# Batch 3's k as token blocks through the DMA's transpose: one change to a fused attention and MoE kernel

## The chip, the cores and the metric

The kernel runs on one core of a Trainium2 chip. The metric is the device time of one execution in microseconds (us). The core has five engines with queues of their own: TensorE (PE; its weight loads are shown as PEld), VectorE (DVE), ScalarE (ACT), GpSimd (POOL) and SyncE (SP), which here only issues DMAs. Each queue runs in order, and engines wait for one another through semaphores.

## What is computed

```python
def _attn_ref(q, k, v):                      # 8 batches, 8 heads, 576 tokens, 64 wide
    scores = scale * np.matmul(q, k.transpose(0, 1, 3, 2))
    rel = pos[:, None] - pos[None, :]
    bias = slopes[:, None, None] * (-np.abs(rel))[None, :, :]
    mask = (rel >= 0) & (rel < 128)
    scores = np.where(mask, scores + bias[None], -1e9)
    attn = softmax(scores)
    return np.matmul(attn, v)

def _moe_ref(x, w_in, w_out):                # 4608 tokens, 512 -> 2048 -> 512
    h = x @ w_in
    g = h * np.clip(h + 3.0, 0.0, 6.0) / 6.0
    return g @ w_out

x = attn_out.transpose(0, 2, 1, 3).reshape(B * S, H * D)
return _moe_ref(x, w_in, w_out)
```

Attention has a causal window of 128 tokens and a linear bias for each head. Its output, heads side by side, goes through two dense layers with a hard swish between them. Inputs and output are float32; the kernel computes its products in bfloat16.

## The kernel before

**Groups.** Attention is worked off in 32 groups: group g is the batch g // 4 and a pair of heads, g % 4 (`hp` in the code). For each group the 576 tokens are cut into five blocks of 128 (the last has 64), and only the scores of a block with itself (`scd`, line 324) and with the block before it (`sco`, lines 350 and 356) are computed. ScalarE takes the exponentials (lines 379, 389, 395) into `pd` and `po`, GpSimd zeroes what lies outside the mask (the selects of lines 382, 392, 398), TensorE multiplies with v (lines 411 and 419, `values`), and VectorE divides by the sums into `avs` (line 430). `back` brings the average into the layout of the dense layers, `xT`: from group 8 on by a DMA transpose that SP issues (line 466), in groups 10 and 11 and before group 8 by TensorE.

**The dense layers as filling.** The dense layers' matmuls (`hps`, line 492, and `ops`, line 547) stand in one list of units, and `fill(n)` puts the next n units between the steps of attention. All engines' orders are written out by hand: `first_batch` (groups 0 to 3), `second_batch` (4 to 7), then `segment` for groups 8 to 32. An iteration g of `segment` holds, in TensorE's order, the scores of group g, units, the averages of group g - 1 in two parts with units between and behind, and the output tiles of finished units are stored by SP (line 557). The scores of group 13 come at the end of iteration 12.

**How q and k get their layout.** The scores need q and k with the head's 64 elements on the partitions (`qTb`, `kTb`, two buffers each, by the batch's parity). There are two ways.
- *Long runs and TensorE.* `load_double` (line 98) loads four heads as runs of nine tokens for each partition (2304 bytes in one piece), in two DMAs of 288 KB; `prepare_double` (line 239) casts them to bfloat16 in two casts of 576 columns; `double` (line 254) transposes the nine pieces on TensorE, five and four, and a copy each (line 256) takes them from PSUM to `kTb`. A batch's k needs this twice (`dp` 0 and 1).
- *Token blocks and the DMA.* `load_tokens` (line 110) loads the five blocks of 128 tokens (8 heads, pieces of 256 bytes; four DMAs of 256 KB and one of 128), `cast_tokens` (line 206) casts each block on GpSimd into the shared buffer `tbuf`, and `xbar` (line 211) lets one DMA transpose of SP's write all of `qTb` or `kTb`. There is one `tbuf`, so the casts of the next tensor wait until the transpose before has read it.

Batches 0 to 2 take the first way for q and k, batches 4 to 7 the second. Batch 3 takes the second for q and the first for k. Its loads are issued by SP at the end of `second_batch`, behind v2's. v3 follows in iteration 9 (`LOADS`), q4 in iteration 10, k4 in iteration 12 and v4 in iteration 13.

**The order around the change.** `stage_next(g)` runs near the end of iteration g and prepares the next batch: it issues the loads of `LOADS`, and in the first two groups of a batch (`hp` 0 and 1) the casts on GpSimd and the transposes on SP. GpSimd's selects for group g + 1 stand behind the casts of `stage_next(g)` in its queue. In iterations 10 and 11 `turn` puts `double` for batch 3's k ahead of the first units.

The four fp32 buffers `ldbuf` are shared: k's runs of batch 3 and its token blocks after the change both lie in buffer 1, q's blocks in buffer 3, v's in buffer 0.

Of the kernel before, what the change touches and what calls it, by code (L numbers as in the profile page):

```python
# [18 lines left out]
def kernel(  # L19
# [9 lines left out]
    nc = tc.nc  # L29
    B, H, S, D = q.shape  # L30
# [5 lines left out]
    NP = H // 2  # L36
# [59 lines left out]
    def load_double(b, dp, nm, eng):  # L96
        for e in range(2):
            eng.dma_start(out=ldbuf["qk".index(nm)][:, ds((2 * dp + e) * RT * D, RT * D)],
                          in_=src_of[nm][b, ds(4 * dp, 4), :, :].rearrange(
                              "(i e) (a t) d -> e a i (t d)", e=2, t=RT)[e])  # L100
# [7 lines left out]
    def load_block(b, nm, j, eng):  # L108
        n = min(128, S - j * 128)
        eng.dma_start(out=tokens(b, nm)[:n, j, :, :],  # L110
                      in_=src_of[nm][b, :, ds(j * 128, n), :].rearrange("h p d -> p h d"))

    def load_tokens(b, nm):
        for j in range(NQ):
            load_block(b, nm, j, nc.sync)
# [79 lines left out]
    def cast_tokens(b, nm):  # L195
        s = ld[b, nm]
        if nm == "v":
            for lo in (0, 2):
                nc.gpsimd.tensor_copy(  # L199
                    out=vbuf[b % 2][:, lo:lo + 2, :, 0:D].rearrange("p j h d -> p (j h) d"),  # L200
                    in_=s[:, lo:lo + 2, :, :].rearrange("p j h d -> p (j h) d"))
            nc.gpsimd.tensor_copy(out=vbuf[b % 2][:LAST, 4, :, 0:D], in_=s[:LAST, 4, :, :])
            return
        for j in range(NQ):
            m = min(128, S - j * 128)
            nc.gpsimd.tensor_copy(out=tbuf[:m, :, j, :],  # L206
                                  in_=s[:m, j, :, :].rearrange("p (i e) d -> p i (e d)", e=2))

    def xbar(b, nm):
        dst = (qTb if nm == "q" else kTb)[b % 2]  # L210
        nc.sync.dma_start_transpose(out=dst.rearrange("p h j c -> p (h j) c"),
                                    in_=tbuf.rearrange("p h j c -> p (h j c)"))
# [22 lines left out]
    def prepare_double(b, dp, copies, nms="kq", early=None):  # L235
        for nm, copy in zip(nms, copies):
            pr = prs.tile([128, RT, 2 * D], BF16, tag=f"pr{nm}", name="pr2")
            for e in range(2):
                copy(out=pr[:, :, ts(e, D)],  # L239
                     in_=ldbuf["qk".index(nm)][:, ds((2 * dp + e) * RT * D, RT * D)].rearrange(  # L240
                         "p (t d) -> p t d", t=RT))
                if early and (nm, e) == (nms[0], 0):
                    early()
            st[b, dp, nm] = pr
# [3 lines left out]
    def double(b, dp, nm, part, tag, copy):  # L248
        src = st[b, dp, nm]
        t0, t1 = ((0, 5), (5, RT))[part]  # L250
        tp = BANKS[tag].tile([128, t1 - t0, 128], BF16, tag=tag, name="tp2",
                             padded_shape=[128, 8, 128])
        for t in range(t0, t1):
            nc.tensor.transpose(tp[:, t - t0, :], src[:, t, :], ident)  # L254
        dst = (qTb if nm == "q" else kTb)[b % 2][:, 2 * dp:2 * dp + 2, :, :]
        copy(out=dst.rearrange("p i j c -> p i (j c)")[:, :, 0:S].rearrange(
                 "p i (a t) -> p i a t", t=RT)[:, :, :, t0:t1],
             in_=tp.rearrange("p t (a i) -> p i a t", i=2))
# [54 lines left out]
    def scores_diag(g):  # L313
        rooms(g)
        b, hp = divmod(g, NP)
        qT, kT = qTb[b % 2][:, hp, :, :], kTb[b % 2][:, hp, :, :]
        first = not diag_tabled(g)
        if (g, "scd") not in st:
            tables_diag(g)
        scd = st[g, "scd"]  # L320
        for j in range(4):
            for e in range(2):
                r = slice(e * D, (e + 1) * D)
                nc.tensor.matmul(scd[:, e, ts(j, 128)], lhsT=kT[r, j, :],  # L324
                                 rhs=qT[r, j, :], start=first, stop=first or j == 3)
# [36 lines left out]
    def exp_off_full(g):  # L362
        nc.scalar.activation(out=st[g, "po"].rearrange("p e j c -> p e (j c)"),
                             in_=st[g, "sco"], func=ACT.Exp, scale=scale)
# [214 lines left out]
    V, P, A = nc.vector.tensor_copy, nc.gpsimd.tensor_copy, nc.scalar.copy  # L579
# [6 lines left out]
    def stage_next(g):  # L586
        b, hp = divmod(g, NP)
        nb = b + 1
        if g == 2 * NP:
            cast_tokens(2, "v")  # L590
        for n in LOADS.get(g, "").split():
            load_tokens(int(n[1]), n[0])
        if nb == 3 and hp < 2:
            prepare_double(3, hp, (P,), "k")
        if nb == 3 and hp == 1:
            cast_tokens(3, "q")
            xbar(3, "q")
        elif nb < B and nb > 3 and hp < 2:
            cast_tokens(nb, "qk"[hp])
            xbar(nb, "qk"[hp])  # L600
        if VCAST.get(g):
            cast_tokens(VCAST[g], "v")
# [76 lines left out]
    def second_batch():  # L679
        scores_diag(NP + 0)  # L680
        exp_diag(NP + 0, 0)
        exp_diag(NP + 0, 1)
        fill(2)
        scores_off(NP + 0)
        exp_off_full(NP + 0)
        wide_double(1, 1, "k", V)
        fill(1)
        wide_double(1, 1, "q", V)
        fill(1)
        scores_diag(NP + 1)  # L690
        exp_diag(NP + 1, 0)
        exp_diag(NP + 1, 1)
        fill(2)
        scores_off(NP + 1)
        exp_off_full(NP + 1)
        fill(1)
        cast_tokens(1, "v")
        scores_diag(NP + 2)
        exp_diag(NP + 2, 0)
        exp_diag(NP + 2, 1)  # L700
        fill(1)
        scores_off(NP + 2)
        exp_off_full(NP + 2)
        fill(2)
        for i in range(0, 4):
            load_w_out(i)
        g = 2 * NP - 1
        scores(g)
        exp_diag(g, 0)
        exp_diag(g, 1)  # L710
        prepare_double(2, 0, (V, P))
        prepare_double(2, 1, (P, P))
        nc.gpsimd.memset(ldbuf[2][:, 0:1], 0.0)
        load_tokens(2, "v")
        for dp in range(2):
            load_double(3, dp, "k", nc.sync)
        load_tokens(3, "q")
        exp_off_full(g)
        fill(1)
        attend(NP)  # L720
        fill(1)
        attend(NP + 1)
        fill(1)
        back(NP)
        attend(NP + 2)
        fill(1)
        back(NP + 1)
        double(2, 0, "k", 0, "av", A)
        attend(NP + 3)
        back(NP + 2)  # L730
        double(2, 0, "k", 1, "av", A)
        wide_double(2, 0, "q", A)
        up_begin(1, 0, 3)
        back(2 * NP - 1)
        up_begin(1, 1, 3)
        done[0] = 2 * NP
        fill(2)
        scores_diag(2 * NP)
        scores_off(2 * NP)
# [3 lines left out]
    def segment(lo, hi, fills):  # L743
        for g in range(lo, hi + 1):
            f = fills(g)
            if by_xbar(g - 2):
                done[0] = g - 1
            if lo < g < hi and g != 3 * NP + 1:
                scores(g)
            turn = {2 * NP: (2, 1, "k"), 2 * NP + 1: (2, 1, "q"),  # L750
                    2 * NP + 2: (3, 0, "k"), 2 * NP + 3: (3, 1, "k")}.get(g)
            if turn:
                double(*turn, 0, "av", A)
            fill(f[0])
            if turn:
                double(*turn, 1, *(("h", V) if turn[0] == 2 else ("av", A)))
            if g < hi:
                exp_diag(g, 0)
            fill(f[1])
            if g < hi:  # L760
                exp_diag(g, 1)
            if g == 3 * NP:
                cast_tokens(3, "v")
            if g > lo:
                values(g - 1, (0, 1, 2))
            fill(f[2])
            if g < hi:
                exp_off(g, 0)
            fill(f[3])
            if g < hi:  # L770
                exp_off(g, 1)
            if g > lo:
                values(g - 1, (3, 4))
            fill(f[4])
            if g > lo and by_xbar(g - 1):
                back(g - 1)
            fill(f[5])
            if g < hi:
                stage_next(g)
            fill(1)  # L780
            if g == 3 * NP:
                scores(g + 1)
            if g > lo and not by_xbar(g - 1):
                back(g - 1)
                done[0] = g
            fill(f[6] - 1)
# [49 lines left out]
```

## Time and profile before

| | |
|---|---|
| median of 3 runs | 323.95 us (323.73 to 324.63) |
| span of the profiled execution | 321.8 us |
| TensorE busy | 308.2 us, 96% |
| ScalarE busy | 196.0 us, 61% |
| VectorE busy | 175.5 us, 55% |
| GpSimd busy | 138.4 us, 43% |
| granted TensorE clock | 0.9 or more in every slice |
| DMA packets | 131426, of which 118977 under 512 bytes |

The profile is that of one execution, and its span is some 2 us shorter than the median of the times, since what lies ahead of the first instruction and behind the last is not in it. Busy times overlap: their sum says nothing, and matmuls are pipelined, so that TensorE's busy time is no measure of how well it is used. A DMA has three times: when SP begins to issue it, when SP is done issuing (only then does SP go on to the next), and when its data has landed. The chain that ended last is followed back from the last instruction and tells which work set the end of this execution; it doesn't tell how close another chain was.

### The profile page before, as it was taken

Reading aid. Unit: us, or ns where it says so; the run is one execution under the profiler, and the core shown is the slowest. Engines: PE = TensorE matmul, PEld = TensorE weight load, DVE = VectorE, ACT = ScalarE, POOL = GpSimd, SP = SyncE. Lnnn points to the kernel's source line nnn. Section 1 sums busy time; section 2 is a strip of 40 time slices with the busy share of each in tenths; the row PEclk is TensorE's granted clock in tenths of the full one; section 3 lists DMA queues with packets and bytes.
Section 4 is the critical chain, followed back from the end, with each engine's and each line's share of the span. In section 5 each row is a group of like instructions: output and inputs, shape, how many; then the busy total and the mean of one; then the engine's idle time right before and its main releaser. Section 6 shows DMA issues by size and latency. Waiting matters only on the chain.

```text
span 321.8 us, 6865 instructions
## 1 busy us (share of the span) xinstructions
PE 308.2 (96%) x2620; PEld 164.6 (51%) x2659; DVE 175.5 (55%) x346; ACT 196.0 (61%) x337; POOL 138.4 (43%) x247
## 2 busy tenths in 40 slices
PE   6888999999999999999999999999999999999996
PEld 3564465455555545455667655455454444444443
DVE  6686595564346655555555556554655455445510
ACT  3857977877777766766676667666764344244401
POOL 7364590665494767446654663663331000000000
PEclk9999999999999999999999999999999999999999
DMA  7999999899999999999799999922011200000112
GB/s 273 262 369 210 269 233 214 235 200 189 201 256 170 242 200 189 204 202 230 179 214 207 211 189 202 236 66 89 20 55 59 80 34 34 33 33 35 65 49 83
DMA packets 131426, 52.43 MB, mean 163 GB/s; under 512 B 118977, under 2 KB 122817, under 8 KB 131393
## 3 DMA queue, kind: packets, MB, share of 16 engines
q1 hardware_dynamic: 125648, 46.15, 67.0%
q0 software_dynamic: 3696, 3.67, 7.0%
q10 hardware_dynamic: 2048, 2.16, 2.2%
q8 instruction: 21, 0.34, 0.5%
q14 instruction: 13, 0.10, 0.1%
HBM read 36.70 MB, written 9.44 MB: 143 GB/s over the span
## 4 chain that ended last, share of the span: by engine, by line
PE 83%; DMA 7%; ACT 4%; issue 2%; DVE 2%; POOL 1%; SPq 0%; ACTq 0%; DVEq 0%
PE ops L547 37%; PE hps L492 35%; DMA gbuf<-in_moe_w_in_dram 3%; PE scd L324 2%; DMA w_in_sb<-in_moe_w_in_dram 2%; PE av L419 2%; DMA ldbuf<-in_k_dram 2%; PE av L411 2%; ACT r L516 2%; PE sco L356 1%; PE ops L528 1%; DVE gbuf L517 1%; PE tp L254 1%; ACT gbuf L379 1%; ACT xT L479 1%
## 5 line engine op out<-in xcount | busy, mean ns | idle before, releaser
L517 DVE SCALAR_TENSOR_TENSOR gbuf<-r,hps 128x512 bf16<-128x512 f32 x144 | 98.5, 687 | 102.3 <-ACT r L516 99.4
L516 ACT ACTIVATE r<-hps,bias 128x512 f32<-128x512 f32 x144 | 98.8, 690 | 90.4 <-PE hps L492 89.3
L492 PE MATMUL hps<-xT,w_in_sb 128*128 128x512 bf16 (+1 forms) x622 | 143.3, 357 | 2.3 <-DMA w_in_sb<-in_moe_w_in_dram 0.9
L547 PE MATMUL ops<-w_out_sb,gbuf 128*128 128x512 bf16 x539 | 134.0, 379 | 2.4 <-issue 1.7
L492 PEld LDWEIGHTS <-w_in_sb 128*128 128x128 bf16 x640 | 59.0, 98 | 55.3 <-issue 1.7
L547 PEld LDWEIGHTS <-gbuf 128*128 128x128 bf16 x560 | 52.2, 98 | 56.9
L382 POOL TENSOR_SCALAR_AFFINE_SELECT pd<-pd 128x512 bf16<-128x512 bf16 x48 | 29.5, 631 | 37.8 <-ACT pd L379 37.7
L392 POOL TENSOR_SCALAR_AFFINE_SELECT po<-po 128x512 bf16<-128x512 bf16 x48 | 30.1, 633 | 32.6 <-ACT po L389 32.4
L556 DVE COPY osb<-ops 128x512 f32<-128x512 f32 x33 | 22.7, 688 | 22.0 <-PE ops L547 21.9
L379 ACT ACTIVATE pd<-scd,bias_d 128x512 bf16<-128x512 f32 x48 | 31.5, 684 | 4.7 <-PE scd L324 4.7
L389 ACT ACTIVATE po<-sco,bias_o 128x512 bf16<-128x512 f32 x48 | 33.1, 690 | 0.0
L206 POOL CAST tbuf<-ldbuf 128x512 bf16<-128x512 f32 (+1 forms) x45 | 25.5, 611 | 17.1 <-issue 17.1
L430 DVE TENSOR_TENSOR avs<-av,rc 128x384 bf16<-128x384 f32 (+1 forms) x48 | 23.6, 491 | 1.6
L419 PEld LDWEIGHTS <-pd 128*128 128x128 bf16 x192 | 14.3, 97 | 7.9 <-issue 0.5
L411 PE MATMUL av<-vbuf,po 128*128 128x65 bf16 x192 | 18.0, 193 | 0.0
L419 PE MATMUL av<-vbuf,pd 128*128 128x65 bf16 x192 | 17.3, 194 | 0.0
L411 PEld LDWEIGHTS <-po 128*128 128x128 bf16 x192 | 14.3, 98 | 2.9 <-DVE avs L430 0.5
L395 ACT ACTIVATE p4buf<-sco,bias_d 128x64 bf16<-128x64 f32 x48 | 15.6, 325 | 0.0
L199 POOL CAST vbuf<-ldbuf 128x1024 bf16<-128x1024 f32 x14 | 14.2, 1041 | 2.4 <-DMA ldbuf<-in_v_dram 2.4
L324 PEld LDWEIGHTS <-kTb 64*128 64x128 bf16 x256 | 7.3, 94 | 14.3 <-issue 10.0
L324 PE MATMUL scd<-qTb,kTb 64*128 64x128 bf16 x256 | 12.7, 219 | 1.9 <-ACT kTb L232 1.2
L239 POOL CAST pr<-ldbuf 128x576 bf16<-128x576 f32 x18 | 11.5, 671 | 2.0 <-DMA ldbuf<-in_k_dram 1.9
(107 smaller groups left out, 216.7 us busy)
## 6 DMA issues: line engine op xcount, KB each, us to landing
out_dram<-osb SPq DMA_DIRECT2D x33, 256.0 KB, 2.5
ldbuf<-in_v_dram SPq DMA_DIRECT2D x31, 256.0 KB, 5.0
ldbuf<-in_q_dram SPq DMA_DIRECT2D x20, 256.0 KB, 4.8
ldbuf<-in_k_dram SPq DMA_DIRECT2D x16, 256.0 KB, 4.6
ldbuf<-in_q_dram SPq DMA_DIRECT2D x12, 288.0 KB, 6.4
ldbuf<-in_k_dram SPq DMA_DIRECT2D x12, 288.0 KB, 6.7
w_out_sb<-in_moe_w_out_dram POOLq DMA_DIRECT2D x4, 512.0 KB, 10.0
w_in_sb<-in_moe_w_in_dram POOLq DMA_DIRECT2D x3, 512.0 KB, 8.6
```

The costliest lines, as they stand in the source:

```text
L206: nc.gpsimd.tensor_copy(out=tbuf[:m, :, j, :], in_=s[:m, j, :, :].rearrange("p (i e) d -> p i (e d)", e=2))
L324: nc.tensor.matmul(scd[:, e, ts(j, 128)], lhsT=kT[r, j, :], rhs=qT[r, j, :], start=first, stop=first or j == 3)
L379: nc.scalar.activation(out=pd[:, e, :, :].rearrange("p j c -> p (j c)"), in_=sc[:, e, :], func=ACT.Exp, bias=bias_d[:, h:h + 1], scale=scale)
L382: nc.gpsimd.affine_select(out=pd[:, e, :, :], in_=pd[:, e, :, :], pattern=[[0, 4], [1, 128]], channel_multiplier=-1, base=0, compare_op=AL ...
L389: nc.scalar.activation(out=po[:, e, :, :].rearrange("p j c -> p (j c)"), in_=sc[:, e, :], func=ACT.Exp, bias=bias_o[:, h:h + 1], scale=scale)
L392: nc.gpsimd.affine_select(out=po[:, e, :, :], in_=po[:, e, :, :], pattern=[[0, 4], [-1, 128]], channel_multiplier=1, base=-1, compare_op=A ...
L411: nc.tensor.matmul(out_av, lhsT=po[:, e, qt % 4, :], rhs=vb[:, qt - 1, h, :], start=True, stop=False)
L419: nc.tensor.matmul(out_av, lhsT=d, rhs=vb[:, qt, h, :], start=(qt == 0), stop=True)
L492: nc.tensor.matmul(hps[:, lo:hi], lhsT=w_in_sb[:, ks, ts(ms, 128)], rhs=xT[:, ks, ds(src, hi - lo)], start=(ks == 0), stop=(ks == n_ks - 1))
L516: nc.scalar.activation(out=r6, in_=hps, func=ACT.Relu, bias=bias3[:, 0:1], scale=1.0 / 6.0)
L517: nc.vector.scalar_tensor_tensor(out=gts[nt][:, ms, :], in0=r6, scalar=1.0, in1=hps, op0=ALU.min, op1=ALU.mult)
L547: nc.tensor.matmul(ops[nt, sub], lhsT=gts[nt][:, ms, ts(sub, 128)], rhs=w_out_sb[:, ms, :], start=(ms == 0), stop=(ms == n_ms - 1))
```

## The change

Batch 3's k is loaded as five token blocks behind q's, where four DMAs of long runs stood ahead of q's. Batch 3 then runs through the same code as batches 4 to 7: q is cast and transposed in iteration 8, k in iteration 9. Before, k's casts stood in both, and q's casts and transpose in iteration 9. `double` in iterations 10 and 11, its 18 transposes and its four copies by ScalarE are gone.

```diff
@@ stage_next
-        if nb == 3 and hp < 2:
-            prepare_double(3, hp, (P,), "k")
-        if nb == 3 and hp == 1:
-            cast_tokens(3, "q")
-            xbar(3, "q")
-        elif nb < B and nb > 3 and hp < 2:
+        if 3 <= nb < B and hp < 2:
             cast_tokens(nb, "qk"[hp])
             xbar(nb, "qk"[hp])
@@ second_batch
         load_tokens(2, "v")
-        for dp in range(2):
-            load_double(3, dp, "k", nc.sync)
         load_tokens(3, "q")
+        load_tokens(3, "k")
         exp_off_full(g)
@@ segment
-            turn = {2 * NP: (2, 1, "k"), 2 * NP + 1: (2, 1, "q"),
-                    2 * NP + 2: (3, 0, "k"), 2 * NP + 3: (3, 1, "k")}.get(g)
+            turn = {2 * NP: (2, 1, "k"), 2 * NP + 1: (2, 1, "q")}.get(g)
             if turn:
                 double(*turn, 0, "av", A)
             fill(f[0])
             if turn:
-                double(*turn, 1, *(("h", V) if turn[0] == 2 else ("av", A)))
+                double(*turn, 1, "h", V)
```

SP's queue from v2's loads on, before: k3 (4 issues), q3 (5), output, averages of group 8, v3 (5), transpose of q3, output, averages of group 9, q4 (5), three outputs, k4 (5), transpose of q4. After: q3 (5), k3 (5), transpose of q3, output, averages of group 8, v3 (5), transpose of k3, output, averages of group 9, q4 (5), three outputs, k4 (5), transpose of q4. GpSimd's queue, before: v2's casts, two casts of k3, selects of group 9, two casts of k3, five casts of q3, selects of group 10. After: v2's casts, five casts of q3, selects of group 9, five casts of k3, selects of group 10.

## The prediction, made before the changed kernel ran

> **What bounds the kernel now.** I read the page first (busy times and the chain that ended last), then the chain through the groups of batch 2 (58 to 84 us), then the queues of SP, GpSimd and TensorE over the same stretch and on to 114 us.
>
> ```profile
> span 321.8 us, 6865 instructions
> PE 308.2 (96%) x2620; PEld 164.6 (51%) x2659; DVE 175.5 (55%) x346; ACT 196.0 (61%) x337; POOL 138.4 (43%) x247
> PE 83%; DMA 7%; ACT 4%; issue 2%; DVE 2%; POOL 1%; SPq 0%; ACTq 0%; DVEq 0%
> ```
>
> TensorE is busy 96% of the span and is 83% of the chain, so an instruction taken off TensorE in mid-run shortens the run, as long as TensorE never waits for anything else. The 321.8 us are one profiled execution, 2.15 below the median of 323.95; I add changes to the median.
>
> ```profile
> 70.69 0.39 PE tp L254 x5
> ...
> 71.93 0.37 PE tp L254 x4
> ```
>
> These are the transposes of k3 in group 10, on the chain; the same two rows come again at 78.69 and 79.94 in group 11. The change removes all four.
>
> ```profile
> 58.68 2.52 SPq L98 DMA_DIRECT2D ldbuf<-in_k_dram  x4
> 61.24 6.14 SPq L110 DMA_DIRECT2D ldbuf<-in_q_dram  x5
> 67.48 0.57 SPq L557 DMA_DIRECT2D out_dram<-osb  x1
> 70.18 2.03 SPq L466 DMA_TRANSPOSE xT<-avs  x1
> 72.27 4.29 SPq L110 DMA_DIRECT2D ldbuf<-in_v_dram  x5
> 76.74 3.63 SPq L211 DMA_TRANSPOSE qTb<-tbuf  x1
> ...
> 82.78 5.47 SPq L110 DMA_DIRECT2D ldbuf<-in_q_dram  x5
> 88.35 2.72 SPq L557 DMA_DIRECT2D out_dram<-osb  x3
> 91.12 4.52 SPq L110 DMA_DIRECT2D ldbuf<-in_k_dram  x5
> 95.82 4.73 SPq L211 DMA_TRANSPOSE qTb<-tbuf  x1
> ```
>
> Start and length of each issue on SP. The queue is nearly full: between 58.68 and 95.82 it waits only 2.13 us (for group 8's averages, before 70.18), 0.52 (before 81.52) and 1.36 (before 90.74, for an output tile). One DMA transpose of tbuf holds SP for 3.63 to 4.73 us.
>
> ```profile
> 102.66 2.83 POOL L206 CAST tbuf<-ldbuf 128x512 bf16<-128x512 f32 x5 [4.36 <-issue]
> 105.45 1.21 POOL L382 TENSOR_SCALAR_AFFINE_SELECT pd<-pd 128x512 bf16<-128x512 bf16 x2
> 106.62 1.21 POOL L392 TENSOR_SCALAR_AFFINE_SELECT po<-po 128x512 bf16<-128x512 bf16 x2
> ```
>
> ```profile
> 107.91 0.23 PE L419 MATMUL av<-vbuf,pd 128*128 128x65 bf16 x2
> ```
>
> This is what matters most. GpSimd stood 4.36 us before k4's casts, because tbuf still held q4 until its transpose landed (issued 95.82, landed 102.55). Group 14's selects queue behind the casts and end at 107.83; TensorE reads them from 107.91. The same holds once more: the transpose of k4, issued 106.32, landed at 113.76, and group 16's scores begin at 113.81. So in batch 3's groups the chain SP, tbuf, GpSimd, TensorE has no slack, though the chain that ended last names only TensorE.
>
> **The change, part by part.**
>
> *Removed from TensorE:* 18 transposes. The gap from one group's scores to the next is 8.01 us with them (70.06 to 78.07) and 7.25 without, under the same fill counts (98.37 to 105.62). So 0.76 a group, 1.52 in all, the sum of the four rows (0.39 + 0.37, twice). On the path: -1.52, if nothing waits.
>
> *Removed from ScalarE:* four copies of 0.76 and 0.73 us, 2.98 in all. From 65.41 to 114 the chain holds TensorE alone and ScalarE, at 61%, is no link of it: 0.
>
> *GpSimd:* four casts of 0.66 us go, 2.6 in all, and five into tbuf come (2.84 as one row): +0.2, under waits. But q3's casts move up a group, to 63.87. v2's last block landed at 61.68; q3 landed at 70.80 behind k's four runs, which took from 61.68 to 65.41. Without them q3 lands 3.73 earlier, at 67.1, and its casts, following the blocks, end at 67.7. Queued behind are group 9's selects (1.22 + 1.22 + 0.29), done at 70.5; TensorE wants them at 73.12 - 0.76 = 72.36. Cover: 1.9 us; if the loads come later than that, the rest is a stall.
>
> *SP and the DMAs.* k3's four issues (288 KB in runs) become five (token blocks), and one 3.65 us transpose is added. In sequence after, from 58.68, with the 0.05 to 0.1 between issues: q3 and k3. Their two series took 10.0 together for batch 4 (5.47 + 4.52) and 10.9 for batch 5 (5.26 + 5.59); I take 10.5, since back to back they are held to the pace of the drain. End 69.2. Transpose of q3 at 69.3, 3.65, to 72.95. Output, averages of group 8 (now ready, so 1.22 and no wait), v3 (4.3): 79.3. Transpose of k3 at 79.4 to 83.05. Output and group 9's averages: 85.0. q4 (5.47): 90.5. Three outputs without their wait (1.6): 92.1. k4 (4.52): 96.65. Transpose of q4: 96.8, against 95.82. So +1.0. As a balance: 1.8 for loads, 3.65 for the transpose and 0.3 for gaps come in, 4.0 of waits and 0.8 of the long issue at 70.18 go out.
>
> *Three waits that this makes, in time.* (1) The transpose of q3 lands 5.2 to 6.7 after its issue (rows at 128.14 and 95.82): 74.5 to 76.0. k3's casts wait there, end 77.3 to 78.8, and group 10's selects behind them end 79.8 to 81.3. TensorE wants them at 81.12 - 1.52 = 79.6: a stall of 0.2 to 1.7; I take 0.7, which leaves -0.8. (2) The transpose of k3 lands 5.65 (row at 76.74) to 7.44 (row at 106.32) after 79.4: 85.05 to 86.85. Group 12's scores, at 86.36 in the trace, now want it at about 85.5: 0 to 1.3; I take 0.4, which leaves -0.4. (3) The transpose of q4, issued 1.0 late, lands at 103.55 if it takes the 6.73 of its own row; k4's casts, group 14's selects and TensorE follow one behind the other without slack. TensorE resumes 1.0 later than in the trace, whatever it had won before: +1.0. The transpose of k4 slips by the same 1.0 and then meets a TensorE that is as late. Past group 16 the trace has slack (batch 5's k lands at 144.99, its scores begin 146.27), so nothing is won or lost further on.
>
> Sum: not -1.52 but +1.0, so 323.95 + 1.0 = 325.0. The bounds of (3): with q3 and k3 at 10.0 and a landing 5.2 after issue, -1.0 before the PE term stops it; with both new transposes at 4.73 and v3 at 5.58 (row at 165.82), +1.0 + 2.2 + 1.3 at worst, of whose 3.5 I keep a third, since long issues are the rarer ones (two of the first five transposes): +2.2.
>
> The Trainium skill, page "DMA: Bandwidth & Descriptors", section "Issuing engines are not separate DMA queues", holds that the sequencer's time to start a DMA is usually small beside the DMA. By that rule SP's added issue time would not matter; the trace differs for these transposes, whose issue is 3.63 to 4.73 of the 5.14 to 7.44 us to landing.
>
> **The rivals.**
>
> *Full gain (faster).* The place is the landing of q4's transpose; if it comes by 102.55 - 1.52 = 101.03, wait (3) takes nothing. For it: load series vary (q6 took 4.44 at 144.93, k7 4.30 at 187.56, and k4's own landing, 4.75 after the end of its issue, is the longest of all; 2.84 to 3.46 later on). With q4 at 4.44 and q3 and k3 at 10.0 the issue is at 95.3, and the shortest landing (5.14, row at 171.50) gives 100.4. Waits (1) and (2) then have to be short as well. Against: every one of these must fall well. It gives 323.95 - 1.5 = 322.4. The page's rule named above would lead here, by the drain alone.
>
> *Part of the gain.* q4's transpose lands near 102, and waits (1) and (2) set the end: -0.4 to -1.2, about 323.2. For it: the landing lag of 4.75 came behind three outputs, which will lie differently. Against: SP's sum.
>
> *A pile-up (slower still).* k3's transpose, with both issues at 4.73 and v3 at 5.58, starts at 81.8 and lands 7.44 later, 89.2, so group 12's scores are 2.9 late: 326.8. Against: three long rows at once.
>
> *The change does nothing:* k3's loads and casts ran beside work anyway and TensorE's 1.52 is met by an equal wait: 323.95.
>
> **How the numbers follow.** About 0.97 us (0.3%) is what a measurement of this kernel can tell from no change: below 322.98 is faster, above 324.92 slower. The forecast, SP's backlog deciding at q4's transpose: 0.58, its own range 323.9 to 326.2, some 0.36 of it above 324.92 and 0.22 within. Full gain 0.18, faster. Part of the gain 0.17: 0.05 faster, 0.12 within. Pile-up 0.05, slower. Nothing 0.02. So faster 0.23, same 0.36, slower 0.41. The range reaches down to the full gain and up to the forecast's top: 322.3 to 326.3.
>
> **What would show it.** No transposes at L254 in groups 10 and 11, and group 10's scores to group 11's in 7.25 if no wait takes its place. On SP: the transpose of q3 at 69.3, of k3 at 79.4, q4's loads from 85.0 and its transpose at 96.8. On GpSimd: idle time before k3's casts until the landing at 74.5 to 76. On TensorE: idle before group 10's averages, group 12's scores, and most of all group 14's averages. I am wrong if q4's transpose is issued at or before 95.8, if its landing ends nobody's wait, or if q3's casts delay group 9.

## The result

The changed kernel takes 325.67 us in the median of 11 runs (324.65 to 327.86), the kernel before 323.95 (323.44 to 324.69): a ratio of 1.006, 95% interval 1.0042 to 1.0077. It is slower by 1.7 us. Its times also lie further apart (3.2 us against 1.3).

First the page of the changed kernel: the span, TensorE's row, the DMA packets and the chain that ended last.

```profile
span 326.1 us, 6871 instructions
PE 311.2 (95%) x2641; PEld 163.7 (50%) x2641; DVE 176.2 (54%) x346; ACT 193.5 (59%) x333; POOL 138.5 (42%) x248
DMA packets 138128, 53.07 MB, mean 163 GB/s; under 512 B 126192, under 2 KB 130032, under 8 KB 138096
PE 65%; issue 2%; POOL 1%; DVE 0%; DMA 0%; POOLq 0%
```

These are 6,702 packets more than before: 7,215 more under 512 bytes, nearly all from k3's blocks and its transpose, and 513 fewer large ones, since k3's long runs are gone. The two spans can't be compared as if both executions were typical: this one took 327.86 us, the slowest of the 11 and 2.19 above their median, while that of before took 323.73, 0.22 below its own. It also starts 1.1 us later: group 8's scores stand at 52.70 against 51.58. I therefore compare distances inside the trace, and totals by the medians. The sizes that this trace gives are those of the slowest run; no other execution of the changed kernel was profiled.

SP's queue of the changed kernel, start and length of the issues:

```profile
65.04 5.78 SPq L110 DMA_DIRECT2D ldbuf<-in_k_dram  x5
70.99 4.56 SPq L211 DMA_TRANSPOSE qTb<-tbuf  x1
...
77.56 4.62 SPq L110 DMA_DIRECT2D ldbuf<-in_v_dram  x5
82.29 3.84 SPq L211 DMA_TRANSPOSE kTb<-tbuf  x1
...
95.03 5.62 SPq L110 DMA_DIRECT2D ldbuf<-in_k_dram  x5
100.83 4.52 SPq L211 DMA_TRANSPOSE qTb<-tbuf  x1
```

The transpose of q4 is issued at 100.83, in the trace of before at 95.82: 3.9 later when the 1.1 of the start is taken off. On GpSimd the casts of k3 and of k4 both wait for the transpose ahead of them, which landed 5.9 and 6.5 us after its issue, at 76.9 and 107.3:

```profile
77.00 2.83 POOL L206 CAST tbuf<-ldbuf 128x512 bf16<-128x512 f32 x5 [4.84 <-issue]
...
107.43 2.83 POOL L206 CAST tbuf<-ldbuf 128x512 bf16<-128x512 f32 x5 [6.51 <-issue]
```

And TensorE, in time order, with the idle time ahead of an instruction and what ended it in brackets:

```profile
80.71 0.19 PE L419 MATMUL av<-vbuf,pd 128*128 128x65 bf16 x1
81.06 0.20 PE L419 MATMUL av<-vbuf,pd 128*128 128x65 bf16 x1 [0.16 <-POOL pd L382]
81.64 0.20 PE L411 MATMUL av<-vbuf,po 128*128 128x65 bf16 x1 [0.38 <-POOL po L392]
...
82.23 0.20 PE L411 MATMUL av<-vbuf,po 128*128 128x65 bf16 x1 [0.35 <-POOL po L392]
...
85.01 0.19 PE L411 MATMUL av<-vbuf,po 128*128 128x65 bf16 x1
...
89.14 0.40 PE L324 MATMUL scd<-qTb,kTb 64*128 64x128 bf16 x8 [1.72 <-DMA kTb<-tbuf]
...
108.39 0.40 PE L324 MATMUL scd<-qTb,kTb 64*128 64x128 bf16 x8
...
110.91 0.20 PE L419 MATMUL av<-vbuf,pd 128*128 128x65 bf16 x1
...
115.45 0.19 PE L411 MATMUL av<-vbuf,po 128*128 128x65 bf16 x1
```

Up to 85.01 these are the averages of group 10, whose first part is released select by select; at 89.14 stand the scores of group 12, released by the landing of k3's transpose; the last three rows are group 14's scores and the starts of its averages' two parts. The third wait lies between those two parts, and the chain of the changed kernel runs through it:

```profile
110.26 1.17 POOL pd L382 x2
111.44 0.49 POOL po L392
...
112.67 0.20 PE av L411
```

The averages of group 14 stand on the chain behind GpSimd's selects. The same instructions in the kernel before:

```profile
81.12 0.22 PE L419 MATMUL av<-vbuf,pd 128*128 128x65 bf16 x2
...
84.02 0.19 PE L411 MATMUL av<-vbuf,po 128*128 128x65 bf16 x1
...
86.36 0.40 PE L324 MATMUL scd<-qTb,kTb 64*128 64x128 bf16 x8
...
105.62 0.40 PE L324 MATMUL scd<-qTb,kTb 64*128 64x128 bf16 x8
...
107.91 0.23 PE L419 MATMUL av<-vbuf,pd 128*128 128x65 bf16 x2
...
110.80 0.19 PE L411 MATMUL av<-vbuf,po 128*128 128x65 bf16 x1
```

By distances between the same instructions in both traces, group 10 loses 1.40 us (4.30 from the first part of its averages to the second against 2.90), group 12 1.79 (4.13 from there to the scores against 2.34), group 14 1.87 (2.51 and 4.54 against 2.29 and 2.89). Together 5.06; less the 1.52 of the transposes that is 3.5, and the two traces differ by 3.42 from group 8 to the last averages of the run. Behind group 16 the distances are the same again. The median run loses less than this profiled one; how its loss is shared among the three waits is not known.

### The profile page after: what moved, and what is told of

Read it like the earlier page. It is cut to its first block, busy times and chain, and to the rows that moved or that the text cites. A ratio compares the mean times of both kernels' runs of the same rounds, so it can differ in the third digit from the quotient of the medians.

```text
span 326.1 us, 6871 instructions
## 1 busy us (share of the span) xinstructions
PE 311.2 (95%) x2641; PEld 163.7 (50%) x2641; DVE 176.2 (54%) x346; ACT 193.5 (59%) x333; POOL 138.5 (42%) x248
## 4 chain that ended last, share of the span: by engine, by line
PE 65%; issue 2%; POOL 1%; DVE 0%; DMA 0%; POOLq 0%
PE ops L547 30%; PE hps L492 27%; PE av L419 2%; PE scd L324 2%; PE av L411 1%; PE ops L528 1%; PE sco L356 1%; POOL tbuf L206 1%; POOL pd L382 0%; POOL po L392 0%; PE sco L350 0%; DVE osb L531 0%; DMA qTb<-tbuf 0%; POOLq L206 0%; POOLq L382 0%
## 5 line engine op out<-in xcount | busy, mean ns | idle before, releaser
L492 PE MATMUL hps<-xT,w_in_sb 128*128 128x512 bf16 (+1 forms) x640 | 145.1, 358 | 1.8 <-DMA w_in_sb<-in_moe_w_in_dram 1.2
L547 PE MATMUL ops<-w_out_sb,gbuf 128*128 128x512 bf16 x560 | 138.0, 380 | 0.0
L206 POOL CAST tbuf<-ldbuf 128x512 bf16<-128x512 f32 (+1 forms) x50 | 28.5, 611 | 26.4 <-issue 24.8
L419 PE MATMUL av<-vbuf,pd 128*128 128x65 bf16 x192 | 18.2, 194 | 0.6 <-POOL pd L382 0.5
L429 DVE RECIPROCAL rc<-av 128x6 f32<-128x6 f32 (+1 forms) x48 | 8.7, 182 | 8.9 <-PE av L419 8.9
```

The costliest lines, as they stand in the source:

```text
L206: nc.gpsimd.tensor_copy(out=tbuf[:m, :, j, :], in_=s[:m, j, :, :].rearrange("p (i e) d -> p i (e d)", e=2))
L419: nc.tensor.matmul(out_av, lhsT=d, rhs=vb[:, qt, h, :], start=(qt == 0), stop=True)
L492: nc.tensor.matmul(hps[:, lo:hi], lhsT=w_in_sb[:, ks, ts(ms, 128)], rhs=xT[:, ks, ds(src, hi - lo)], start=(ks == 0), stop=(ks == n_ks - 1))
L547: nc.tensor.matmul(ops[nt, sub], lhsT=gts[nt][:, ms, ts(sub, 128)], rhs=w_out_sb[:, ms, :], start=(ms == 0), stop=(ms == n_ms - 1))
```

## The experiments

Each ran beside the kernel before on the same chip. Theory A was that SP's queue is late, rival B that the single buffer tbuf is.

**What TensorE gains.** Everything for batch 3's k left out.

```diff
-        load_tokens(3, "k")
-        if 3 <= nb < B and hp < 2:
+        if 3 <= nb < B and hp < 2 and (nb, hp) != (3, 1):
             cast_tokens(nb, "qk"[hp])
             xbar(nb, "qk"[hp])
```

> The changed kernel without anything for batch 3's k: no loads, no casts, no DMA transpose; group 12 to 15 read the k that lies in the buffer from batch 1. It is the bound of what taking the 18 transposes off TensorE can give. If the 1.52 us of the prediction are right, 322.4 us; if TensorE's transposes were hidden anyway, 323.95. No wait is expected in groups 10, 12 and 14 beyond those of the kernel before.

322.42 us, ratio 0.9957 (0.9943 to 0.9971): 1.52 below the 323.94 of its neighbours, the size worked out from four rows of the chain. SP is relieved here too: counted from group 8's scores, q4's transpose goes out 1.6 us sooner than in the kernel before. So this is what TensorE gains when SP keeps up with it. What the change loses elsewhere is 325.67 - 322.42 = 3.25 us.

**Loads or transpose?** Four of k3's five loads left out, then its transpose alone.

```diff
-        load_tokens(3, "k")
+        load_block(3, "k", 4, nc.sync)
```

> The changed kernel with four of the five loads of batch 3's k left out (the casts read what lies in the buffer). Theory A, SP's queue is what is late: SP reaches the transpose of q3 some 4 us sooner, so all three waits shrink to little: 322.4 to 323.3. Rival B, the single buffer tbuf is what is late (k's casts wait for q's transpose whenever it starts, and q's casts set that): the transpose of q3 starts when q3's casts end, only 1 to 1.5 us sooner, and the waits of groups 10 and 14 mostly stay: 324.5 to 325.5.

```diff
             cast_tokens(nb, "qk"[hp])
-            xbar(nb, "qk"[hp])
+            if (nb, hp) != (3, 1):
+                xbar(nb, "qk"[hp])
```

> The changed kernel without the DMA transpose of batch 3's k (the scores read the k of batch 1 that lies there); loads and casts stay. Theory A: the wait of group 10 stays as it is (about 1.4 us in the trace), that of group 12 is gone, and SP is 3.8 us sooner at q4, so that of group 14 is gone too: 323.5 to 324. Rival B: the same for group 12, but the wait of group 14 for k4's casts stays, 324.5 to 325.

Without the loads 324.91 (ratio 1.0026, 1.0007 to 1.0045), without the transpose 323.21 (0.9978, 0.9964 to 0.9992). The loads alone give back 0.76, the transpose 2.46; the sum, 3.22, is about the whole loss. The first lies where B had put it, the second below where A had; so theory A missed the worth of the loads. In the trace without the transpose TensorE waits in group 10 alone, as A had it. GpSimd's casts of k3 and of k4 without the loads:

```profile
74.06 2.83 POOL L206 CAST tbuf<-ldbuf 128x512 bf16<-128x512 f32 x5 [2.87 <-DMA qTb<-tbuf]
...
103.52 2.83 POOL L206 CAST tbuf<-ldbuf 128x512 bf16<-128x512 f32 x5 [5.96 <-DMA qTb<-tbuf]
```

Groups 10 and 12 no longer lose anything, but k4's casts still wait 5.96 and group 14 still loses 1.5: one transpose more ahead of q4's (with the one load of 128 KB that was kept) is enough for that.

**A buffer of its own for k's casts.**

```diff
-    tbuf = held.tile([128, NP, NQ, 128], BF16, name="tbuf")
+    tbufs = [held.tile([128, NP, NQ, 128], BF16, name=f"tbuf{i}") for i in range(2)]
...
+        tbuf = tbufs["qk".index(nm)]
```

> The changed kernel with a buffer of its own for k's casts, in all batches, the result the same. Theory A (SP's queue): GpSimd no longer waits before k3's and k4's casts, so the waits of groups 10 and 14 go, but SP is as late as before and the transpose of k3 lands no sooner: the wait of group 12 grows by what group 10 no longer takes, 324.5 to 325.2. Rival B (the buffer): 322.4 to 323, with no wait left.

325.45 (ratio 1.0048, 1.0031 to 1.0065), little above A's 324.5 to 325.2 and far from B's 322.4 to 323. Two rows of its waits: who waited for whom, us in total, times, longest (lines lie 3 further down, L327 is the scores):

```profile
PE scd L327 <- DMA kTb<-tbuf: 2.3, 1, 2.3
POOL tbuf L208 <- DMA ldbuf<-in_k_dram: 2.2, 2, 1.6
```

Groups 10 and 14 lose nothing any more, as meant, and group 12 waits longer for the transpose of k3, 2.3 us against 1.72. The wait has moved, not gone. Rival B falls.

**Moving v3's loads out of the way**, alone and with the second buffer.

```diff
+            if n != "v3":
...
             xbar(nb, "qk"[hp])
+        if g == 9:
+            load_tokens(3, "v")
```

> The changed kernel with one thing moved: v3's five loads are issued behind the transpose of k3 instead of ahead of it. Theory A (SP's queue makes the transposes late): the transpose of k3 then starts when k3's casts end, about 2.5 us sooner, and group 12's wait (1.7 us in the trace) goes; those of groups 10 and 14 stay: 323.7 to 324.4. Rival C, what is late in group 12 is the moving of the data and not SP's order: 325.4 to 326.

> The changed kernel with a buffer of its own for k's casts and with v3's loads behind the transpose of k3. Theory A: the buffer takes the waits of groups 10 and 14, the order on SP that of group 12, and only TensorE's gain is left: 322.4 to 323.2, as without any k3. If the waits are one shortage of DMA bandwidth that moves on to another place, 324.5 or more.

Both missed widely: 330.41 (ratio 1.0187, 1.0157 to 1.0217) and 328.61 (1.0123, 1.0092 to 1.0154). Group 12's wait is gone in both, and in the second group 10's and group 14's too. What came in their place is a long one. For the version with the order alone, a row of the table by stages: start and end, length, busy time of PE, PEld, DVE, ACT and POOL, granted clock, DMA share, GB/s.

```profile
76.00:80.00 4.00, 3.91 (x35) 1.86 (x33) 2.04 (x5) 1.63 (x4) 4.00 (x8) 1.00 0.15 30
```

SP stands 2.98 us before the transpose of k3, for its casts, with v3's loads queued behind it, and the DMAs are all but idle (0.15). In the changed kernel the 4.62 us of v3's loads filled this time. They are paid for in group 14, whose averages wait 3.37 us for one select, and there the clock stands at 0.5 for 6.83 us. With the buffer as well, SP doesn't stand; TensorE, in time order:

```profile
113.43 1.03 PE L495 MATMUL hps<-xT,w_in_sb 128*128 128x512 bf16 x4
118.16 0.40 PE L327 MATMUL scd<-qTb,kTb 64*128 64x128 bf16 x8 [3.71 <-DMA kTb<-tbuf]
...
119.88 1.91 PE L495 MATMUL hps<-xT,w_in_sb 128*128 128x512 bf16 x4
```

TensorE comes without a wait from group 10 to group 16's scores and there stands 3.71 us, for the transpose of k4. Behind that, four matmuls take 1.91 instead of 1.03 us. The table by stages of the same run shows why, in its third figure from the right:

```profile
112.00:116.00 4.00, 2.45 (x12) 0.90 (x10) 2.58 (x5) 2.40 (x5) 3.00 (x5) 1.00 1.34 236
116.00:120.00 4.00, 1.84 (x23) 1.06 (x24) 0.00 (x0) 0.69 (x1) 0.97 (x2) 0.91 0.91 161
120.00:124.00 4.00, 4.00 (x23) 1.90 (x22) 1.35 (x3) 2.05 (x4) 0.89 (x3) 0.66 1.18 231
```

After the wait TensorE's granted clock was halved for 3.41 us. So this wait cost more than its own 3.71 us: about half of 3.41 came on top.

**Two controls.** The kernel before with q3's loads ahead of k3's, and with one transpose more.

```diff
+        load_tokens(3, "q")
         for dp in range(2):
             load_double(3, dp, "k", nc.sync)
-        load_tokens(3, "q")
```

> The kernel before with only the order of the loads as in the change: q3's blocks ahead of k3's runs. k3's first runs then land near 69 us instead of 63, and GpSimd's casts of them wait and end near 70, group 9's selects behind them near 72.5, just ahead of TensorE at 73.1. Theory A: no difference, 323.6 to 324.3. If the order of the loads is a cost of its own: 324.5 to 325.5.

```diff
             xbar(3, "q")
+            xbar(3, "q")
```

> The kernel before with one more DMA transpose on SP: that of q3 is issued a second time into the same place. Nothing else is added, and TensorE's transposes of k3 stay. It measures what one transpose more on SP costs by itself. Theory A: 3.7 us of issue against about 1.9 us of SP's waits that can take it, so q4's transpose is some 1.8 us late and group 14 waits: 325.3 to 326.2. If SP's issue time costs nothing, 323.95.

The order of the loads makes no difference (324.1, ratio 0.9994, 0.9979 to 1.001). The second transpose costs about 2.9 us: 327.15 against 324.28 (1.0109, 1.0067 to 1.0152), more than the 325.3 to 326.2 expected. Part of the surplus belongs to the experiment: the second, into the same place, waited 1.4 us for the first to land. In the profiled execution (331.27, the slowest of six) TensorE's clock was halved once besides, from 114.1 to 117.5 us. That is not what makes the median: a halved stretch of 3.41 us takes 0.005 off the mean clock of a run of this length, and the three runs with a mean clock of 0.999 or 1.0, which leaves no room for one, took 326.68 to 326.98.

**SP's issue time or the DMAs' moving of data?** Five output stores of groups 8 to 13 issued by ScalarE, in the changed kernel, with the second buffer as well, and in the kernel before.

```diff
-                nc.sync.dma_start(out=out[rows, :], in_=osb)
+                if 8 <= now[0] <= 13:
+                    late.append((at[0], rows, osb))
...
+            while late and late[0][0] < at[0]:
+                _, rows, osb = late.pop(0)
+                nc.scalar.dma_start(out=out[rows, :], in_=osb)
```

> The changed kernel with the five output stores of groups 9 to 13 issued by ScalarE instead of SP, one unit after their tile is copied. SP loses some 2.8 us of issue between v2's loads and q4's transpose; the bytes that the DMAs move stay the same. Theory A1, SP's issue time is what is late: the waits of groups 12 and 14 shrink by about that, 323.0 to 324.2. Theory A2, the DMAs' draining of many small pieces is what is late and SP only waits for it: 325.2 to 326. A cost by ScalarE standing still at the stores would add to either.

> The same with a buffer of its own for k's casts as well. Theory A1: the waits of groups 10 and 14 go with the buffer and that of group 12 shrinks by SP's relief: 322.6 to 323.6, below the kernel before. Theory A2: as with the second buffer alone, 325 to 325.6.

> The kernel before with the same five stores issued by ScalarE, as a control: what the moved stores cost or give where no wait of SP ends in TensorE. 323.6 to 324.3 if they are free; more by what ScalarE's standing still costs.

325.88 (ratio 1.0054, 1.0037 to 1.0072), 327.76 (1.01, 1.0065 to 1.0134), and the control 324.6 (1.0006, 0.9993 to 1.0019). By the times that is A2 for the first. In its trace groups 12 and 14 lose nothing any more, as A1 had it; group 10 loses more, and then the clock falls (stages of the first version):

```profile
80.00:84.00 4.00, 2.47 (x18) 1.05 (x17) 1.57 (x4) 2.83 (x6) 4.00 (x9) 0.93 1.28 241
84.00:88.00 4.00, 4.00 (x20) 1.69 (x19) 0.60 (x2) 0.00 (x0) 1.22 (x3) 0.65 1.16 169
```

TensorE stood 1.53 of the 4 us in four waits, and twelve output matmuls behind them took 4.44 us where the changed kernel's took 2.75. But the clock is not the whole account: three of the six runs had a mean clock of 0.999, so no halved stretch, and took 325.45 to 325.96 all the same; where they lost it is not known, since none of them was profiled. The second version has 3.4 us of wait before group 12's scores and a halved clock for 6.8 us. Its one run with a mean clock of 0.999 took 325.27, which is A2's number. The question was not settled this way.

**Taking work out of the stretch.** The second buffer, v3's loads behind, and output stores of groups 9 to 13 put off by SP to groups 15 and later, with eight output tiles instead of four to hold them. Four stores were held, where the expectation says five.

```diff
-    opool = ctx.enter_context(tc.tile_pool(name="opool", bufs=4))
+    opool = ctx.enter_context(tc.tile_pool(name="opool", bufs=8))
...
-                nc.sync.dma_start(out=out[rows, :], in_=osb)
+                if 9 <= now[0] <= 13:
+                    late.append((rows, osb))
...
+            if late and g >= 15:
+                rows, osb = late.pop(0)
+                nc.sync.dma_start(out=out[rows, :], in_=osb)
```

> The changed kernel with a buffer of its own for k's casts, v3's loads behind the transpose of k3, and the five output stores of groups 9 to 13 put off by SP to one in each of groups 15 to 19 (eight output tiles instead of four). The one thing new against the version with buffer and order alone (328.61 us) is that five stores, some 2.8 us of SP's issue and as much moving of data, leave the stretch up to q4's and k4's transposes. If what the change added is a debt of the DMAs that is paid at whichever wait comes next, the long wait of group 16 shrinks by about that and TensorE's clock is not halved behind it: 322.8 to 324.5, perhaps below the kernel before. If the debt is only carried on to batch 5, or a moved transpose is what is slow, 325.5 or more.

323.66 (ratio 0.9974, 0.9958 to 0.9991): 5.0 below the same version without the delay, 2.0 below the changed kernel, and by its interval a little below the kernel before. SP's queue there:

```profile
97.62 4.84 SPq L214 DMA_TRANSPOSE qTb<-tbuf  x1
...
108.68 3.81 SPq L214 DMA_TRANSPOSE kTb<-tbuf  x1
```

The start is 0.85 earlier than in the changed kernel; apart from it q4's transpose goes out 2.4 us sooner and k4's 1.6. The waits of groups 10, 12, 14 and 16 are all gone. One new wait of TensorE is left in the profiled execution (325.07, the slowest of its twelve): group 11's averages stand behind VectorE, which waited for the transpose of group 9's to land before it wrote the same buffer:

```profile
PE av L414 <- DVE avs L433: 1.9, 1, 1.9
```

Whether the delayed stores would also help the kernel before was not tried, so this version doesn't show that k3's new way is the better one. Nor were the eight output tiles tried by themselves.

## Why the prediction was right, and where it was too small

- *TensorE's 1.52 us:* measured as 1.52, by leaving out all of k3, with SP relieved as well.
- *ScalarE's copies, put at nothing:* the chain before is not quite TensorE's alone from 65.41 to 114; between 90.0 and 92.3 us it runs through VectorE and through one copy of ScalarE's (0.65 us). The four copies that go lie ahead of that, in groups 10 and 11, so the 0 stands.
- *q3's casts a group earlier:* with the start taken off, the casts end at 68.4 (67.7 forecast) and group 9's averages don't wait. Right.
- *The three waits:* all three came, at the places named, in the forecast order and released by what was named (selects behind casts behind a landing; a landing; again the first). Leaving the transpose out shows that it is the larger part, 2.46 of 3.25; the second buffer shows that the wait moves when its place is taken away. In the profiled execution, the slowest of 11, they took 1.40, 1.79 and 1.87 us, where the sum had 0.7, 0.4 and 1.4.
- *What was mis-sized:* SP's sum, "Transpose of q4: 96.8, against 95.82. So +1.0". In the profiled execution it is 3.9. The terms: q3 and k3 took 11.3 instead of 10.5, the transpose of q3 4.56 instead of 3.65, v3 and k3's transpose 0.5 more, averages and waits 1.1 more, k4 1.1 more, q4 1.2 less, and q3 began 0.35 earlier. I had taken the issue times as fixed prices, and they vary: a transpose of tbuf held SP for 3.09 us where the DMAs had been all but idle before it (v3's loads moved behind) and for 3.84 to 4.56 in the changed kernel, five loads for 4.25 to 5.78. That they lengthen with the DMAs' backlog fits the 3.09, but was not tested by itself. Accordingly q3's landing fits (75.8 after taking off the start, forecast 74.5 to 76.0), k3's is late (88.0, forecast 85.05 to 86.85), and so is q4's (106.2, forecast 103.55). The 3.9 is more than a usual run would show: in the version with the second buffer, which has the same order on SP and whose profiled execution (325.17) lies near its median, q4's transpose is 2.7 late.
- *The total:* +1.0 forecast, +1.7 by the medians, +3.4 from group 8 on between the two profiled executions. The forecast's own range, 323.9 to 326.2, holds seven of the eleven runs, the median among them; the other four lie above it.
- *"TensorE resumes 1.0 later than in the trace, whatever it had won before":* the mechanism holds, with another number. In the profiled execution, with the start taken off, k4's casts begin 3.65 us later than before (107.43 against 102.66), and the second part of group 14's averages comes 3.53 later (115.45 against 110.80), although groups 10 and 12 had already lost 3.19 and the transposes had won 1.52.
- *The rule of the Trainium skill* (page "DMA: Bandwidth & Descriptors", section "Issuing engines are not separate DMA queues") that a sequencer's time for issuing is usually small beside the DMA: it does not hold for these transposes, whose issue was 4.56, 3.84 and 4.52 us of the 5.9, 6.8 and 6.5 to landing in the changed kernel. Whether SP's issue time therefore decides was not settled. Moving stores to ScalarE took away two waits in the trace, but not time, and taking them out of the stretch took away SP's issue and the DMAs' work together. SP's queue is nearly full (from 59.45 to 105.35 us of the changed kernel its longest pause is 0.51); whether its own issue or the DMAs' work behind it is what falls short stays open.
- *Full gain, the rival on the other side:* only reached without k3's work.

## What to carry to other kernels

When a queue and the DMAs behind it are full, work added to them is a debt that one wait or another collects: here a second buffer or another order only chose which wait, and taking work out of the stretch paid it. Look for the transfers that land at the very moment when they are needed; the chain that ended last doesn't show them, as it named hardly anything but TensorE in this stretch. And before taking load from the busiest engine, ask whether the queue that gets it has as much free time in that same stretch, for 1.52 us won on TensorE cost 3.25 elsewhere.

## What the hardware showed

TensorE's clock ran at full rate from 5.5 us on in the profiled executions of the kernel before and of the changed kernel. After waits it was halved in those of six of the twelve experiments, for 3.41 us or twice that (stretches at 0.5 that began at 83, 88, 92, 111, 114 and 119 us); in two others it was halved once at 8 us, in the kernel's start. By half of its length, a halved stretch of 3.41 us costs about 1.7 us of TensorE's work. The six runs with ScalarE's stores and the second buffer fit that: 325.27 us at a mean clock of 0.999, 326.84 at 0.994 (one stretch), 327.26 to 329.31 at 0.99 and 0.989 (two).

Where a wait falls matters as well as how long it is. In these traces the full stretches between two changes of the clock last whole multiples of 3.41 us (78.51 us is 23 of them, 112.64 is 33), as if the clock were decided once in each step of 3.41 us. Counted in these steps, from the trace's matmuls, TensorE idle for 1.88, 1.91, 2.29, 2.57 or 3.24 us of one step was followed by half the clock, and idle for 1.72 us of one (the changed kernel, group 12) was not. The wait of 2.3 us in the version with the second buffer lay across two steps, 0.96 and 1.39 us idle, and cost no clock. One case doesn't fit a plain limit: four short waits of 1.53 us in sum were enough.

None of the changed kernel's eleven runs met a halved stretch, since their mean clocks are 0.999 or 1.0. Their spread of 3.2 us has another cause, which no trace shows.

The Trainium skill, page "TensorE: Matmul & The Clock Gate", section "Part 1: The HAM clock gate", puts half rate behind at least one idle window of some 3.4 us. The length of the window agrees with the 3.41 us; that it must be idle throughout doesn't, since TensorE worked for more than half of the 3.41 us before the clock fell in the run with 1.53 us of waits.
